# A fused attention and two-stage MoE kernel: earlier query and key loads, a third raw buffer, later reciprocals, and the larger TensorE budget from step 16

## The chip, the cores and the metric

The kernel runs on one core of a Trainium2 chip. The metric is the device time of one execution in microseconds (us), less is better. PE is TensorE, DVE is VectorE, ACT is ScalarE, POOL is GpSimd, and SP is the engine whose queue issues nearly all transfers.

## The reference, cut to what matters

```python
scores = scale * np.matmul(q, k.transpose(0, 1, 3, 2))      # 4 batches, 8 heads, 576 x 576, depth 64
kth = np.partition(scores, -32, axis=-1)[..., -32:-31]
scores = np.where(scores >= kth, scores, -1e9)
attn = np.exp(scores - scores.max(-1, keepdims=True)); attn /= attn.sum(-1, keepdims=True) + 1e-9
x = heads side by side of np.matmul(attn, v)                # 2304 tokens x 512
x = ((x @ w_a) * (x @ w_b)) @ w_out                         # 512 -> 1536 -> 512
# then top 1 of 8 experts by cosine similarity with expert_emb, softmax gate with tau,
out[tokens of e] = gate * (np.maximum(x @ w1[e], 0) @ w2[e])   # 512 -> 1024 -> 512
```

The weights w_a, w_b and w_out come as 64-bit floats, all else as 32-bit floats.

## The kernel before, in words

Attention is cut into 144 rows of 128 queries. DVE finds the 32 largest of each row's 576 scores with four MAX8 and three MATCH_REPLACE8 (lines 385 and 388). A loop over steps walks over the rows: in each step it writes out the scores of the row two ahead, half of the top-k search of the current row and half of that of the one before it, the softmax of the row two back and the transposes ("turn") of the row three or, from step 19 on, four back. On PE, DVE, ACT and POOL the order of the program is the order of execution; only the SP queue is ordered by priority, where a larger offset goes first.

Rows are grouped into parts: four rows of one pair of heads (256 queries of each), five rows where a batch's last 64 queries go with them, or one such row alone (the four parts "0T", rows 48 to 51). A part loads its queries (and, when it is the first of its batch and pair, its keys), splits them into a high and a low half (`split_k`, `split`), and turns them on PE. When its last row is turned, `mix` multiplies the weights `wt` with the values, and `sums` gives the reciprocals of the row sums: POOL adds 1e-9 (line 428), DVE takes the reciprocal (line 430).

Each part takes two `wt` tiles, one for each head, from `WT` buffers: at its first row's turn the first head's and later the other's. A row of "0T" takes both at once, ahead of the `mix` of the part before it, which stands later in the same step.

The three weight matrices are converted during attention, in 36 blocks (`Blocks`): a load into one of `RB` raw buffers, two DVE operations (lines 532 and 534) and one on ACT (535) that read it, an addition on POOL (539), then two copies on ACT and two products on PE. `start` writes out the first three operations, one block every other step up to step 16 and two in each step from then on, with at most two blocks waiting for POOL; `stage` advances the blocks, three times in a step.

As soon as 256 tokens are mixed, they make a group, and `moe1` computes the first MoE for it: 12 blocks of 24 products of 256 columns (line 683) and 6 of 512 (line 652). Nine groups are worked through in the background of attention: PE gets a budget in each step, in nominal us, from which what attention itself takes is subtracted:

```python
share[0] = max((STEP0 if step < S0 else STEP) - cost, 0.0) / max(n, 1)   # 4.5, 38, 5.4
```

Group 0 can't go past a block of weights that isn't written out yet (`yield None`). A group may begin two steps after its last token is written, group 0 one step after; when no group is due, the budget isn't used. After attention come the rest of the groups and the experts.

Of the kernel before, what the change touches and what calls it, by code (L numbers as in the profile page):

```python
# [16 lines left out]
AF = mybir.ActivationFunctionType  # L17
# [18 lines left out]
F0 = 1  # L36
# [4 lines left out]
ZB = 4  # L41
YB = 2
XG = 1
RB = 2
FOLD = (0,)
PEN = (0,)
PC = 512
# [3 lines left out]
STEP0 = 4.5  # L51
D0 = 1
RD = 2
S0 = 38
RGAP = 2
DEBT = 1.0
SB = 5
# [10 lines left out]
FX = (0, 5)  # L68
EK = 1
EL = 1  # L70
WT = 4
QM = 2
AHEAD_P = 5
AHEAD_Q = 2
FG = 100000
# [7 lines left out]
def fused_kernel(  # L83
# [18 lines left out]
    pe, dve, act, pool, sp = nc.tensor, nc.vector, nc.scalar, nc.gpsimd, nc.sync  # L102
# [6 lines left out]
    NE, _, F2 = w1.shape  # L109
    NP = H // 2  # L110
# [52 lines left out]
    eps = cst.tile([P, 1], F32, name="eps")  # L163
# [5 lines left out]

    enT = cst.tile([P, KC, EW], F32, name="enT")  # L170
    dve.memset(enT, 0.0)

    def en_load(mk):
        e_sb = mk.tile([P, RW], F32, name="xr")[:NE, :DM]
# [23 lines left out]
    with ExitStack() as ph:  # L198
# [60 lines left out]
        def load_v(o):  # L259
            o.vs = wk.tile([P, 2, 5, D], F32, name="vs", bufs=2)  # L260
            h0 = 2 * o.pr
            sp.dma_start(
                o.vs[:, :, 0:4, :].rearrange("p h c d -> p h (c d)"),
                v[o.b, h0 : h0 + 2, 0:512, :].rearrange("h (p c) d -> p h (c d)", c=4),
            )
            sp.dma_start(o.vs[64:128, :, 4, :], v[o.b, h0 : h0 + 2, 512:576, :].rearrange("h s d -> s h d"))
# [158 lines left out]
        def sums(o, add):  # L425
            sl = slice(0 if o.M else 4, 5 if o.tail else 4)
            if add:
                pool.tensor_scalar(o.rc[:, sl], o.sm[:, sl], 1e-9, None, op0=OP.add)
                return
            dve.reciprocal(o.rc[:, sl], o.rc[:, sl])  # L430
# [58 lines left out]
        class Blocks:  # L489
# [9 lines left out]
            def fetch(self, n):  # L499
                while len(self.raw) < min(n, len(self.order)):  # L500
# [5 lines left out]
                    if src.dtype == F32:  # L506
                        raw = mk.tile([P, KC, P], F32, name="raw64", bufs=RB)
                        sp.dma_start(raw, src)
# [269 lines left out]
        rows = []  # L778
# [8 lines left out]
        made = {}  # L787

        live = {}
        NRW = len(rows)  # L790
# [73 lines left out]
        for step in range(-AHEAD_L, NRW + TL + 5):  # L864
            now[0] = step
            if step + AHEAD_L < NRW:
                b, pr, part, first, last, kind, c, slot = rows[step + AHEAD_L]
                if first:
                    with tc.high_priority(offset=FG):
                        o = made[b, pr, part] = prep(b, pr, part, len(made), c0)  # L870
                        coming.append(o)
                    if pr == NP - 1:
                        c0 += o.N
            if 0 <= step + AHEAD_P < NRW:
                b, pr, part, first, last, kind, c, slot = rows[step + AHEAD_P]
                o = made[b, pr, part]
                if first:
                    o.flip = turn_qk(o)
                    flips.append(o)
                    parts.append(o)  # L880
                    o.left = 0
                o.left += 1
                live[step + AHEAD_P] = Rows(o, kind, c, slot)
                live[step + AHEAD_P].n = step + AHEAD_P
            for ahead in (1, -2):
                j = step + ahead
                if 0 <= j < NRW and rows[j][3] and (made[rows[j][:3]].n < 2) == (ahead == 1):
                    with tc.high_priority(offset=FG):
                        load_v(made[rows[j][:3]])
            with tc.high_priority(offset=FG):  # L890
                next(soft, None)
                soft = softmax(live[step - 2]) if 0 <= step - 2 < NRW else none
                for back in (3, 5):
                    j = step - back
                    if 0 <= j < NRW and rows[j][4] and (made[rows[j][:3]].n < F0 * NP) == (back == 3):
                        if back == 3:
                            sums(made[rows[j][:3]], True)
                        sums(made[rows[j][:3]], False)
                j = step - 3
                if 0 <= j < NRW and rows[j][4] and made[rows[j][:3]].n >= F0 * NP:  # L900
                    sums(made[rows[j][:3]], True)
                if 0 <= step < NRW:
                    cur = topk(live[step], FOLD[step % len(FOLD)])
                for _ in range(4):
                    next(thresholds[0], None)
                    next(cur, None)
                if step == NRW:
                    thresholds[0] = none
                elif 0 <= step < NRW:
                    thresholds[0] = cur  # L910
            if step == -AHEAD_L:
                conv.fetch(RB)
            pace = {-5: 1, -1: 2}.get(step, 0) if step < 2 else (step + 1) % 2 if step < 16 else 2
            if step == 4:
                e_sb, e_ss = en_load(mk)
            if step == 12:
                en_norm(e_sb, e_ss)
            if step == 14:
                en_turn(mp, e_sb)
            for o in coming[:1]:  # L920
                if step >= o.first - AHEAD_P or (step >= o.first - AHEAD_P - 2 and not flips):
                    pieces.append(split_qk(o))
                    coming.pop(0)
                    while step < EAGER and pieces:
                        piece()
            while 0 <= step + AHEAD_Q < NRW and live[step + AHEAD_Q].o in flips:
                flip_next()
            i = step - (TL0 if step < S1 else TL)
            if i != turned[0] + 1:
                i = -1  # L930
            else:
                turned[0] = i
            tg = turn(live[i]) if 0 <= i < NRW else none
            sg = scores(live[step + AHEAD_Q]) if 0 <= step + AHEAD_Q < NRW else none
            mg = mixes[0] if mixes else none
            cost, n = 0.0, 0
            if tg is not none:
                cost, n = cost + 0.54, n + 2
            if sg is not none:
                cost, n = cost + (0.96 if live[step + AHEAD_Q].kind == 2 else 0.48), n + 2  # L940
            if mg is not none:
                cost, n = cost + parts_n[0] / 100, n + 1
            if flips:
                cost, n = cost + 0.44, n + 2
            share[0] = max((STEP0 if step < S0 else STEP) - cost, 0.0) / max(n, 1)
            for slot_, g in enumerate((tg, sg, tg, mg, sg)):
                if g is not none and not run(g) and g is mg and mixes:
                    mixes.pop(0)
                    mg = none
                with tc.high_priority(offset=FG):  # L950
                    if slot_ == 1 or slot_ == (2 if mg is not none else 3):
                        next(soft, None)
                    if slot_ < 3 and step >= 0:
                        conv.stage()
                if slot_ in (2, 4):
                    piece()
            if 0 <= step + AHEAD_Q < NRW:
                live[step + AHEAD_Q].o.left -= 1
            for _ in range(2):
                flip_next()  # L960
            if 0 <= i < NRW:
                next(tg, None)
                b, pr, part, first, last, kind, c, slot = rows[i]
                t = live.pop(i)
                if last:
                    while mixes:
                        if not run(mixes[0]):
                            mixes.pop(0)
                    mixes.append(mix(t.o))
                    parts_n[0] = t.o.N  # L970
                    while t.o.n < F0 * NP and mixes:
                        if not run(mixes[0]):
                            mixes.pop(0)
            while not EAGER <= step < NRW and pieces:
                piece()
            for _ in range(pace):
                with tc.high_priority(offset=FG):
                    conv.start()
            while done < len(GROUPS) and sum(GROUPS[done]) <= ready[0]:
                w = step + (D0 if done == 0 else RD)  # L980
                todo.append([w, Group(done, w), None])
                if done and len(todo) < 3 and conv.ready(1, NF - 1):
                    todo[-1][1].inputs()
                    if len(todo) == 1:
                        todo[-1][1].load()
                done += 1
# [322 lines left out]
```

## Time and profile before

| | |
|---|---|
| three runs | 1326.34, 1331.99 and 2752.71 us, median 1331.99 |
| profiled execution | 1326.2 us, its span 1324.5 us, mean granted TensorE clock 0.955 |
| busy | PE 1181.9, DVE 913.1, ACT 821.6, POOL 719.9 us |

The span is what the trace shows, from the first instruction to the last; all times in the trace count from its start. A busy PE is not PE at its peak, since matmuls are pipelined. The granted clock is the share of full speed, 2.4 GHz, that the chip lets TensorE run at. Attention ends at about 890 us.

### The profile page before, as it was taken

Reading aid. Unit: us, or ns where it says so; the run is one execution under the profiler, and the core shown is the slowest. Engines: PE = TensorE matmul, PEld = TensorE weight load, DVE = VectorE, ACT = ScalarE, POOL = GpSimd, SP = SyncE. Lnnn points to the kernel's source line nnn. Section 1 sums busy time; section 2 is a strip of 40 time slices with the busy share of each in tenths; the row PEclk is TensorE's granted clock in tenths of the full one; section 3 lists DMA queues with packets and bytes.
Section 4 is the critical chain, followed back from the end, with each engine's and each line's share of the span. In section 5 each row is a group of like instructions: output and inputs, shape, how many; then the busy total and the mean of one; then the engine's idle time right before and its main releaser. Section 6 shows DMA issues by size and latency. Waiting matters only on the chain. (4 is left out here: it accounts for less than half of the span.)

```text
span 1324.5 us, 23353 instructions
## 1 busy us (share of the span) xinstructions
PE 1181.9 (89%) x7908; PEld 996.1 (75%) x7909; DVE 913.1 (69%) x1995; ACT 821.6 (62%) x1961; POOL 719.9 (54%) x1188
## 2 busy tenths in 40 slices
PE   4766988898999987999998998899999989999996
PEld 3544766677898876888887887677898868888885
DVE  6999999988898986999988898750200135444440
ACT  4777888777777775687777776662532334444441
POOL 4555786766677775767766766564445321111100
PEclk9677999999999997999999998899999989999999
DMA  6334476466695654766765667458988145555520
GB/s 211 118 108 140 159 248 219 164 215 211 202 258 166 187 194 135 209 191 195 194 194 175 204 180 211 135 154 268 324 282 253 32 129 198 174 170 168 177 91 19
DMA packets 129101, 240.56 MB, mean 182 GB/s; under 512 B 24621, under 2 KB 73901, under 8 KB 128978
## 3 DMA queue, kind: packets, MB, share of 16 engines
q1 hardware_dynamic: 124818, 228.74, 55.3%
q0 software_dynamic: 4160, 10.29, 2.4%
q8 instruction: 64, 1.05, 0.3%
q14 instruction: 59, 0.48, 0.1%
HBM read 198.92 MB, written 40.85 MB: 181 GB/s over the span
## 5 line engine op out<-in xcount | busy, mean ns | idle before, releaser
L385 DVE MAX8 t<-y 128x8 f32<-128x576 f32 x432 | 312.0, 750 | 2.9
L400 POOL TENSOR_TENSOR z<-s,z 128x576 f32<-128x576 f32 x144 | 206.0, 1430 | 98.0 <-ACT z L397 95.9
L683 PE MATMUL ab<-xg,wab 128*128 128x256 f32 x1440 | 214.4, 291 | 4.8 <-ACT gab L687 3.1
L388 DVE MATCH_REPLACE8 y<-t,y 128x576 f32<-128x576 f32 x288 | 213.9, 743 | 0.0
L683 PEld LDWEIGHTS ab<-xg,wab 128*128 128x128 f32 x1440 | 189.2, 192 | 8.1 <-ACT gab L687 3.5
L683 PE MATMUL ab<-raw,wab 128*128 128x256 f32 x1152 | 173.4, 292 | 7.2 <-ACT gab L687 4.3
L419 PE MATMUL tr<-ident,z 128*128 128x128 f32 x720 | 137.9, 292 | 41.4 <-ACT z L402 34.7
L683 PEld LDWEIGHTS ab<-raw,wab 128*128 128x128 f32 x1152 | 152.2, 193 | 10.7 <-ACT gab L687 5.0
L402 ACT ACTIVATE z<-z,bi 128x576 f32<-128x576 f32 x144 | 111.4, 774 | 78.2 <-POOL z L400 78.0
L385 DVE MAX8 t<-s 128x8 f32<-128x576 f32 x144 | 107.8, 748 | 59.9 <-ACT s L365 49.0
L364 PE MATMUL tr<-kT,qT 128*128 128x288 f32 x512 | 129.2, 336 | 21.5 <-ACT qT L341 10.9
L422 ACT ACTIVATE wt<-tr 128x384 f32<-128x384 f32 (+2 forms) x320 | 127.3, 412 | 18.5 <-PE tr L419 18.0
L365 ACT ACTIVATE s<-tr 128x288 f32<-128x288 f32 x288 | 118.9, 414 | 30.3 <-PE tr L364 28.7
L652 PE MATMUL x<-wo,gh 128*128 128x512 f32 x432 | 137.7, 400 | 0.0
L419 PEld LDWEIGHTS tr<-ident,z 128*128 128x128 f32 x720 | 92.7, 148 | 56.4 <-ACT z L402 38.8
L1015 DVE TENSOR_TENSOR u<-raw,u 128x1024 fp32r<-128x1024 f32 x64 | 76.3, 1221 | 85.3 <-ACT u L1014 62.5
L639 POOL TENSOR_TENSOR gab<-gab 128x256 f32<-128x256 f32 x108 | 81.5, 754 | 97.0 <-ACT gab L687 92.0
L1064 POOL DMA_INDIRECT out_dram<-o,ids x24 | 23.9, 994 | 201.0 <-ACT o L1063 197.7
L1092 PE MATMUL y<-u,hT 128*128 128x512 f32 (+1 forms) x528 | 128.0, 396 | 0.4 <-DVE hT L1197 0.4
L364 PEld LDWEIGHTS tr<-kT,qT 128*128 128x128 f32 x512 | 90.5, 207 | 37.1 <-ACT qT L341 13.2
L397 ACT ACTIVATE z<-s,bi 128x576 f32<-128x576 f32 x144 | 112.5, 781 | 0.0
L1092 PEld LDWEIGHTS y<-u,hT 128*128 128x128 f32 (+1 forms) x528 | 89.7, 174 | 27.6 <-DVE hT L1197 0.5
(178 smaller groups left out, 2213.8 us busy)
## 6 DMA issues: line engine op xcount, KB each, us to landing
wab<-wab_d SPq DMA_DIRECT2D x192, 512.0 KB, 4.4
raw<-in_moe_w_dram SPq DMA_DIRECT2D x28, 1024.0 KB, 5.1
wab_d<-wab SPq DMA_DIRECT2D x24, 512.0 KB, 3.2
kT<-kT_d SPq DMA_DIRECT2D x20, 576.0 KB, 4.5
vs<-in_v_dram SPq DMA_DIRECT2D x36, 256.0 KB, 3.0
kT_d<-kT SPq DMA_DIRECT2D x16, 576.0 KB, 3.7
raw<-in_moe_w_a_dram SPq DMA_DIRECT2D x12, 512.0 KB, 4.1
raw<-in_moe_w_b_dram SPq DMA_DIRECT2D x12, 512.0 KB, 4.3
```

Source lines behind the costliest of these rows:

```text
L364: pe.matmul(p, l, r, start=(i == 0), stop=(i == len(terms) - 1))
L365: act.activation(t.s[:, cs], p, AF.Copy, scale=SCALE)
L385: dve.max(v, cur)
L388: dve.match_replace(out=rest, in_to_replace=v, in_values=cur, imm_value=LOWEST)
L397: act.activation(t.w, t.s, AF.Relu, bias=t.bi[:, 1:2], scale=-HUGE)
L400: pool.tensor_tensor(t.w, t.s, t.w, op=OP.subtract)
L402: act.activation(t.w, t.w, AF.Exp, bias=t.bi[:, 0:1], accum_out=t.o.sm[:, t.slot : t.slot + 1])
L419: pe.transpose(pt[:, i * P : (i + 1) * P], t.w[:, k0 : k0 + P], ident)
L422: act.activation(th[:, sl, w], pv[:, :, src], AF.Copy)
L652: pe.matmul(px[t], g[:, ts], wo[:, w, f], start=(f == 0 and i == 0), stop=(f == NF - 1 and i == 2))
L683: pe.matmul(p[:, i], wt[:, a, c, :], xg[x][:, c, :], start=(j == 0), stop=(j == len(terms) - 1))
L1092: pe.matmul(p[:m], (hi, lo)[a], u[:, b, f % 4, :], start=(f == 0 and i == 0), stop=(f == NF2 - 1 and i == 2))
```

## The change

- The loads of the first three parts get a higher priority on the SP queue than everything else; the value loads of the first two parts come in step 2 after their first row like all others, not in the step before it.
- An activation with Exp on one element stands near the start of ACT's program.
- `RB` is 3 instead of 2 and `WT` 3 instead of 4.
- In the first four parts the reciprocal on DVE is written out in the middle of the step's top-k operations instead of ahead of them.
- `conv.stage` is called from step 2 on, not from step 0.
- `S0` is 16 instead of 38.

```diff
-RB = 2
+RB = 3
-S0 = 38
+S0 = 16
-WT = 4
+WT = 3
     dve.memset(enT, 0.0)
+    act.activation(enT[:, 0, 0:1], eps, AF.Exp)
...
-                    with tc.high_priority(offset=FG):
+                    with tc.high_priority(offset=max(4 - len(made), 1) * FG):
                         o = made[b, pr, part] = prep(b, pr, part, len(made), c0)
...
-            for ahead in (1, -2):
-                j = step + ahead
-                if 0 <= j < NRW and rows[j][3] and (made[rows[j][:3]].n < 2) == (ahead == 1):
-                    with tc.high_priority(offset=FG):
-                        load_v(made[rows[j][:3]])
+            j = step - 2
+            if 0 <= j < NRW and rows[j][3]:
+                with tc.high_priority(offset=FG):
+                    load_v(made[rows[j][:3]])
...
-                for back in (3, 5):
-                    j = step - back
-                    if 0 <= j < NRW and rows[j][4] and (made[rows[j][:3]].n < F0 * NP) == (back == 3):
-                        if back == 3:
-                            sums(made[rows[j][:3]], True)
-                        sums(made[rows[j][:3]], False)
+                j = step - 5
+                if 0 <= j < NRW and rows[j][4] and made[rows[j][:3]].n >= F0 * NP:
+                    sums(made[rows[j][:3]], False)
                 j = step - 3
-                if 0 <= j < NRW and rows[j][4] and made[rows[j][:3]].n >= F0 * NP:
-                    sums(made[rows[j][:3]], True)
+                summed = made[rows[j][:3]] if 0 <= j < NRW and rows[j][4] else None
+                if summed:
+                    sums(summed, True)
                 if 0 <= step < NRW:
                     cur = topk(live[step], FOLD[step % len(FOLD)])
-                for _ in range(4):
+                for n in range(4):
                     next(thresholds[0], None)
                     next(cur, None)
+                    if n == 1 and summed and summed.n < F0 * NP:
+                        sums(summed, False)
...
-                    if slot_ < 3 and step >= 0:
+                    if slot_ < 3 and step >= 2:
                         conv.stage()
```

## Rows read from the trace of the kernel before

**Rows 1.** The page's 40 slices of the span, DVE and granted clock.

```profile
DVE  6999999988898986999988898750200135444440
...
PEclk9677999999999997999999998899999989999999
```

**Rows 2.** Busy time by stretch: length, then each engine, clock, DMA share, GB/s.

```profile
134.00:249.00 115.00, 99.14 (x601) 75.27 (x601) 107.68 (x225) 95.95 (x213) 86.44 (x101) 0.96 0.60 206
249.00:283.00 34.00, 30.39 (x218) 23.65 (x217) 30.62 (x68) 25.90 (x62) 23.15 (x32) 1.00 0.61 204
283.00:483.00 200.00, 187.01 (x1490) 163.69 (x1489) 180.68 (x417) 150.59 (x407) 141.78 (x262) 1.00 0.67 203
```

**Rows 3.** Timeline of the SP queue's issues, first 10 us.

```profile
0.76 0.44 SPq L512 DMA_DIRECT2D raw<-in_moe_w_a_dram  x1
1.26 0.50 SPq L241 DMA_DIRECT2D kr<-in_k_dram  x1
...
3.37 0.57 SPq L246 DMA_DIRECT2D kr<-in_k_dram  x1
...
5.34 0.60 SPq L246 DMA_DIRECT2D kr<-in_k_dram  x1
5.99 3.62 SPq L228 DMA_DIRECT2D qr<-in_q_dram  x4
```

**Rows 4.** The page's transfers: KB each, median us from issue to landing.

```profile
raw<-in_moe_w_a_dram SPq DMA_DIRECT2D x12, 512.0 KB, 4.1
```

**Rows 5.** Timeline of all engines, up to the first MAX8 and shortly after.

```profile
9.54 1.28 ACT L255 ACT_TABLE_LOAD   x1 [9.41 <-DMA kr<-in_k_dram]
...
11.55 1.00 DVE L256 TENSOR_TENSOR ks<-kr,ks 128x576 fp32r<-128x576 f32 x1 [7.94 <-ACT ks L255]
...
14.00 0.42 DVE L532 TENSOR_SCALAR w64t<-raw 128x512 int32<-128x512 int32 x1
...
17.40 0.76 DVE L385 MAX8 t<-s 128x8 f32<-128x576 f32 x1 [1.33 <-ACT s L365]
...
19.61 2.50 POOL L539 TENSOR_TENSOR x1T<-w64t,w64r 128x512 int32<-128x512 int32 x2
```

**Rows 6.** DVE by line, 17 to 110 us: busy, mean ns, idle before.

```profile
L430 DVE RECIPROCAL rc<-rc 128x4 f32<-128x4 f32 x3 | 0.5, 179 | 5.3 <-POOL rc L428 5.3
```

**Rows 7.** DVE by line, 110 to 275 us.

```profile
L385 DVE MAX8 t<-s 128x8 f32<-128x576 f32 x26 | 19.3, 741 | 0.0
L532 DVE TENSOR_SCALAR w64t<-raw 128x512 int32<-128x512 int32 x27 | 15.3, 567 | 7.2 <-DMA raw<-in_moe_w_b_dram 5.2 <-DMA raw<-in_moe_w_a_dram 1.9
```

**Rows 8.** Busy time by stretch, of instructions on tile ab: PE, PEld, ACT.

```profile
140.00:250.00 110.00, 32.66 (x201) 27.46 (x199) 5.42 (x9) 0.97 0.63 216
250.00:290.00 40.00, 9.53 (x64) 8.23 (x64) 1.79 (x3) 1.00 0.63 213
```

**Rows 9.** Timeline of PE, 338 to 342 us.

```profile
338.77 1.59 PE L683 MATMUL ab<-raw,wab 128*128 128x256 f32 x12
...
341.97 0.62 PE L652 MATMUL x<-wo,gh 128*128 128x512 f32 x2
```

**Rows 10.** DVE by line, 275 to 480 us.

```profile
L385 DVE MAX8 t<-s 128x8 f32<-128x576 f32 x36 | 27.0, 751 | 14.9 <-ACT s L365 11.5 <-POOL z L400 2.0 <-POOL gab L639 1.3
```

**Rows 11.** DVE by line, 482.7 to 527.2 us.

```profile
L385 DVE MAX8 t<-s 128x8 f32<-128x576 f32 x6 | 4.5, 758 | 10.3 <-ACT s L365 10.3
```

**Rows 12.** Busy time by stretch, 500 to 517 us.

```profile
500.00:517.00 17.00, 13.30 (x64) 10.08 (x63) 11.15 (x25) 9.98 (x24) 10.38 (x20) 0.61 0.28 67
```

**Rows 13.** Timeline of PE and ACT in the steps that turn 0T.

```profile
347.59 2.53 PE L460 MATMUL tr<-wt,vs 128*64 128x256 f32 x20
...
348.58 0.53 ACT L422 ACTIVATE wt<-tr 128x192 f32<-128x192 f32 x2
...
353.87 0.55 ACT L422 ACTIVATE wt<-tr 128x192 f32<-128x192 f32 x2
...
355.44 0.89 PE L460 MATMUL tr<-wt,vs 128*64 128x64 f32 x18
...
359.15 0.55 ACT L422 ACTIVATE wt<-tr 128x192 f32<-128x192 f32 x2
...
361.64 0.89 PE L460 MATMUL tr<-wt,vs 128*64 128x64 f32 x18
```

## The prediction

> **What bounds the kernel now.** I read the 40 slices first, then busy time by stretch, and then, for each stretch that the change touches, the DVE rows by line and what ended the idle time before them. The slices show DVE nearly full up to the end of attention, with a dip at the 16th slice where the granted clock dips too [rows 1]. By stretch there are two regimes. From 134 to 249 us DVE is busy 107.7 of 115 us and PE 99.1: DVE sets the pace, because the weight blocks are converted in it, and PE has some 16 us to spare. From 283 to 483 us PE is busy 187.0 of 200 us and DVE 180.7, and DVE's idle time there ends with scores from ACT [rows 2, 10]: PE's queue sets the pace. So a DVE wait that is taken away before about 250 us moves everything behind it earlier, as long as PE keeps up; PE work that is moved counts only where PE is the bound.
>
> **The start.** SP issues in the order of the rows: the three key loads lie behind and between raw weights and values, the last at 5.34 us, and the query loads begin at 5.99 [rows 3]. ACT gets the keys at 9.5 us, loads its table for 1.28 us, copies, and DVE subtracts at 11.55 [rows 5]. With keys and queries first, the three key loads take 0.50, 0.57 and 0.60 us of issue from 0.76 on, so the last begins at 1.83 instead of 5.34 us: 3.5 us earlier, and with the table already loaded the subtraction comes 3.5 + 1.3 = 4.8 us earlier. But what moves back is the raw block. DVE's order has its first operation on raw weights at 14.00 us, ahead of the last copies before the first MAX8 at 17.40 [rows 5]. Behind three key loads (1.67 us) and four query loads (3.62 us) the first raw load is issued at 0.76 + 5.29 = 6.05 us and lands, by the median of its kind, 4.1 us later [rows 3, 4], at 10.15: 3.85 us ahead of 14.00. So the raw weights are late next, and the first MAX8 comes at about 13.5 us. **Term: -3.9 us.** The bounds are -4.8 (the raw lands sooner, the key chain decides) and -2.5 (I allow it 1.4 us more, since the queries and keys are still being moved).
>
> **Loads and stages moved.** The value loads of the first two parts leave the head of the SP queue for step 2 of their part; the first `mix` is four steps later, which hides them. If that cover were gone, the mix would wait one landing, of the size of that in [rows 4], twice. Starting `stage` at step 2 delays the additions and copies of two blocks; nothing needs these blocks before group 0 in step 21. The third block's DVE operation then waits for a free buffer that POOL gives back in step 2; if DVE reaches it first, it loses one addition of about 1.25 us (two take 2.50) [rows 5]. The first three parts' higher priority can hold SP only at a key buffer that the first part hasn't freed, and the loads behind it are needed later. All of this at nothing.
>
> **Reciprocals.** In the first four parts DVE stands still until POOL has added to the row sums: 5.3 us before three of them [rows 6]. Put behind four of the step's DVE operations of 0.74 us each (as a MAX8) [rows 7], some 3 us, the reciprocal finds its input ready, as the three waits are 5.3/3 = 1.8 us in the mean. The order on PE is unchanged: `along`, which reads the reciprocals, stands behind `mix`. **Term: -5.0 us**, between -5.3 and -3, if scores are late next.
>
> **The third raw buffer.** From 110 to 275 us DVE waits 7.2 us for raw weights before line 532, 27 blocks [rows 7], while MAX8 never waits for scores (0.0). A buffer is free when DVE and ACT have both read it, and the next load is written out only then. With three buffers the load goes out one block earlier, and in most steps that is one step earlier, more than its landing of about 4 us. The upper end is all 7.2 us; the lower is nothing, since PE is at 86% in this stretch and gets more to do (next). **Term: -4 us**, the middle.
>
> **The budget from step 16.** Group 0 begins in step 21. I followed the loop's counters through these steps (cost of each generator, share, debt of at most 1, blocks written out): before, its 288 products of 256 columns are all written out by step 39, after by step 35, and the gate `yield None` turns the background away only five times. That 64 of these products lie in the trace behind 250 us, 201 between 140 and 250 [rows 8], agrees with the first count. What moves ahead is then about 64 products and 16 of 512 columns. Twelve of 256 took 1.59 us, 0.12 each with the pipeline's end subtracted, two of 512 took 0.62, some 0.2 each [rows 9]: 7.7 + 3.2 = 11 us of PE. The room for it is the 16 us that PE idles between 134 and 249 [rows 2].
>
> Where it is taken away it gives little. From 249 to 283 us DVE is busy 30.6 of 34 us, so at most 3.4 us can be had there. Behind that the budget of each step is as before; groups 1 and 2 end two steps sooner, but group 1 may not begin before step 40 and group 3 not before step 80, since the attention rows set these dates, and the budget that finds no group is lost. Nor are such steps quick: in the gap ahead of group 3, six steps take 44.5 us, 7.4 each, with DVE idle 10.3 us for scores [rows 11], against 205/36 = 5.7 us a step with the budget in use [rows 10]. So two more empty steps there may cost 2 x 1.7 = 3.4 us. **Term: 0**, from -3.4 to +14 (+3.4, and +10 for a second gap, see the rivals).
>
> **Three wt buffers.** Only 0T's rows take two buffers at once. With three, the second copy of the row must wait for the `mix` of the part before, which PE reaches later. In the trace these copies begin at 348.6, 353.9 and 359.2 us, the first of each pair taking some 0.27, and those mixes end at 350.1, 356.3 and 362.5 [rows 13]: waits of 1.3, 2.2 and 3.1 us, with a fourth row some 9 us of ACT's queue, and behind it the scores for the next row. Scores are made two rows ahead, and ACT is busy three quarters of the time in such steps (150.6 of 200 us) [rows 2], so most is caught up. **Term: +2 us**, from 0 to +6. Four- and five-row parts take their second buffer two rows later, when that mix is done: nothing.
>
> **Sum.** -3.9 - 5.0 - 4 + 0 + 2 = -10.9 us. From the profiled 1326.2 us (span 1324.5 and 1.7 around it) that gives 1315. That run stands 5.8 us below the median of the three runs shown and at their lowest; a median after may stand a little over its fastest too, so I say 1316.
>
> **Rivals.** *The moved work pays in full:* if steps behind 283 us lose 11 us of PE work one for one, because PE is the bound there, the time is 1315 - 11 = 1304. For it speaks PE's 187 of 200 us; against it, that the step's budget stays the same and the gap ahead of group 3 already swallows what is done early. *The emptied gap:* slower. Group 0 ends in step 35 to 38 and group 1 starts in step 40, so there is a new gap of some four steps of the kind in [rows 11]. In that gap's second half the granted clock is 0.61, between its two levels of 1.2 and 2.4 GHz, after PE had been partly idle [rows 12], and the next group starts at the low level. Six steps times 1.7 us is 10 us; with the longer gap ahead of group 3 (+3.4) and the full +6 for 0T, against -12.9 of the first three terms: +6.5, or 1333 us. It decides from the point where the clock falls in the new gap; against it speaks that the four-row parts around step 36 leave PE less of a chain to wait for, and that products of 512 columns trickle on to step 38. The Trainium skill has a rule on this side ("TensorE: Matmul & The Clock Gate", section on HAM oscillation): bursts of matmuls with waits between them let the clock fall back, and every next burst starts cold. The trace agrees at this one gap (0.61); by the rule the time would be this rival's. *The change does not do what it says:* the third buffer brings nothing, as ACT reads the raw block late and PE fills up, scores hold DVE where the reciprocal did (-3), the start gives -2.5 and 0T takes +6: +0.5, 1327 us.
>
> **How the numbers follow.** Forecast 0.50, full payment 0.17, emptied gap 0.18, not what it says 0.15. The range runs from 1302 to 1335: down to just past full payment, and up past the gap, with what is left out at its ends under 0.2. Two per cent, about what can be told from no change here, is 26.6 us of 1332: under 1305 lies half of the full payment, with the other half and the tail of the forecast above it, so 0.08; over 1358 the gap would have to open twice, 0.05; within 0.87.
>
> **What would show it.** The first MAX8 at 13 to 14 us; no idle time before the early reciprocals; the idle time before line 532 under 4 us; group 0's last product of 256 columns at about step 36; ACT waiting on PE before line 422 only around step 52; a granted clock of 1.00 between steps 36 and 41 for the forecast, one under 0.9 for the emptied gap. The prediction is wrong if the raw loads hold DVE much past 10 us, if DVE starts to wait for scores from 134 us on, or if steps in the budgeted stretch take other than 5.7 us.

## The result, and the profile after

The change made the kernel slower: 1336.26 us in the median of six runs beside 1327.8 us of the kernel before, a ratio of 1.0067 [1.0048, 1.0087], in brackets its 95% interval. That is 8.9 us more, where 1316 us was forecast, and just outside the range, which ended at 1335. One of the six runs of before, of 2752.71 us, is left out of the ratio. The profiled execution took 1340.65 us (span 1338.9), 4.4 above that median, so the worth of a whole edit is taken from timed ratios below; lengths of steps come from one trace each and show places.

To see where, I read the times at which steps begin (the MAX8 on `s` opens a step). The shift against before is -3.2 us at step 0, -4.7 at step 22, +6.1 at step 34, +5.6 at 36, +13.3 at 44, +14.2 at 53, +18.0 at 58, +14.0 at 84 and +14.4 at the end. So the loss arises between steps 22 and 58, and nothing behind step 84 plays a visible part.

The 40 slices of the page, after, answer to [rows 1]:

```profile
DVE  7999998879878998899989899760110135444440
...
PEclk8876999978999998999999999799999989999999
```

The clock's dip in the 16th slice is smaller than before (8 for 7), and there is a new one in the 9th, 268 to 301 us (7 for 9); DVE has digits of 7 and 8 in most of slices 7 to 13. Where the time goes is told by stretches. Busy time by stretch, after (length, then PE, PEld, DVE, ACT, POOL, clock, DMA share, GB/s); the first row is that of [rows 2], the second is steps 22 to 34, the others run through steps 37 to 41:

```profile
134.00:249.00 115.00, 98.88 (x602) 72.64 (x602) 105.64 (x206) 92.97 (x201) 84.17 (x96) 0.99 0.60 207
...
140.00:242.90 102.90, 89.53 (x538) 64.11 (x537) 93.64 (x180) 82.77 (x178) 75.88 (x85) 1.00 0.65 227
...
260.00:268.00 8.00, 8.00 (x60) 5.79 (x60) 5.45 (x12) 5.85 (x16) 5.06 (x10) 1.00 0.57 176
268.00:276.00 8.00, 3.43 (x24) 2.87 (x22) 4.89 (x12) 5.13 (x14) 3.92 (x9) 0.95 0.21 83
276.00:281.00 5.00, 4.53 (x18) 3.98 (x18) 5.00 (x13) 3.34 (x9) 3.23 (x10) 0.50 0.67 212
281.00:286.00 5.00, 2.88 (x17) 2.70 (x17) 4.97 (x12) 4.65 (x11) 4.11 (x6) 0.50 0.33 96
286.00:295.00 9.00, 9.00 (x56) 6.21 (x55) 5.61 (x13) 3.60 (x11) 3.12 (x6) 0.65 0.11 29
```

and the same twelve steps of before:

```profile
144.70:236.80 92.10, 77.07 (x471) 56.15 (x470) 84.88 (x176) 78.15 (x171) 70.57 (x80) 0.98 0.67 229
```

In the fixed window 134 to 249 after looks like before (PE 98.9 against 99.1 us), which says only that both kernels work at the same rate there. Taken by steps, the same twelve rows of attention last 102.9 instead of 92.1 us. PE is busy 12.5 us more in them, and its idle time stays: 13.4 us after, 15.0 before. What PE waits for shows in its rows by line, steps 22 to 34, after (busy, mean ns of one, idle before; after's line numbers are one higher than before's):

```profile
L551 PE MATMUL tr<-x1T,ident 128*128 128x512 f32 x48 | 25.8, 618 | 7.8 <-POOL x1T L540 7.7
...
L552 PE MATMUL tr<-wab,minusr 128*128 128x512 f32 x18 | 12.2, 680 | 2.9 <-ACT wab L548 2.8
...
L552 PE MATMUL tr<-wo,minusr 128*128 128x512 f32 x6 | 3.9, 647 | 2.6 <-ACT wo L548 2.6
```

These are the two products of the conversion of a weight block, waiting for POOL's addition and ACT's copy of that block: 13.3 of the 13.4 us. Before, in the same steps, the wait ahead of them is shorter, and PE also waits for the queries that the scores are made from:

```profile
L550 PE MATMUL tr<-x1T,ident 128*128 128x512 f32 x37 | 19.3, 600 | 2.1 <-POOL x1T L539 2.1
L364 PE MATMUL tr<-kT,qT 128*128 128x288 f32 x50 | 12.1, 317 | 4.8 <-ACT qT L341 4.2 <-ACT wt L422 0.7
...
L551 PE MATMUL tr<-wab,minusr 128*128 128x512 f32 x13 | 8.6, 659 | 4.9 <-ACT wab L547 4.9
```

With 1.6 us ahead of the same product for `wo`, the conversion has 8.6 of before's 15.0 us, and other waits have 6.4. So the "16 us to spare" of the prediction were two things. After, the other waits are gone, and those for the conversion have grown by 4.7 us: PE works in program order, and its queue stands behind a product whose input isn't ready, whatever else is written out behind it.

DVE's conversion rows in the same stretch, after:

```profile
L535 DVE TENSOR_SCALAR w64r<-raw 128x512 int16<-128x512 int16 x22 | 18.9, 860 | 0.0
L533 DVE TENSOR_SCALAR w64t<-raw 128x512 int32<-128x512 int32 x22 | 18.4, 836 | 9.2 <-POOL x1T L540 6.8 <-DMA raw<-in_moe_w_b_dram 2.4
```

Beside [rows 7], raw weights hold DVE little now (2.4 us); it waits for POOL instead, and one operation of line 533 takes 0.836 us where it took 0.567 (0.603 in these twelve steps alone).

### The profile page after: what moved, and what is told of

Read it like the earlier page. It is cut to its first block, busy times and chain, and to the rows that moved or that the text cites. A ratio compares the mean times of both kernels' runs of the same rounds, so it can differ in the third digit from the quotient of the medians.

```text
span 1338.9 us, 23347 instructions
## 1 busy us (share of the span) xinstructions
PE 1187.8 (89%) x7908; PEld 998.4 (75%) x7909; DVE 921.8 (69%) x1995; ACT 820.1 (61%) x1962; POOL 721.1 (54%) x1188
## 5 line engine op out<-in xcount | busy, mean ns | idle before, releaser
L684 PE MATMUL ab<-xg,wab 128*128 128x256 f32 x1440 | 210.9, 289 | 5.5 <-ACT gab L688 3.4
L423 ACT ACTIVATE wt<-tr 128x384 f32<-128x384 f32 (+2 forms) x320 | 127.6, 412 | 27.7 <-PE tr L420 18.8
L420 PEld LDWEIGHTS tr<-ident,z 128*128 128x128 f32 x720 | 93.1, 149 | 57.2 <-ACT z L403 37.7
```

The source lines that it names most:

```text
L420: pe.transpose(pt[:, i * P : (i + 1) * P], t.w[:, k0 : k0 + P], ident)
L423: act.activation(th[:, sl, w], pv[:, :, src], AF.Copy)
L684: pe.matmul(p[:, i], wt[:, a, c, :], xg[x][:, c, :], start=(j == 0), stop=(j == len(terms) - 1))
```

## The experiments

The first theory was that the budget from step 16 (S0) alone loses the time, in the conversion of weights or in the gap it opens between groups 0 and 1; the rivals were the third raw buffer and the third `wt` buffer. Step starts (us) of the runs that are spoken of, worked out from the MAX8 rows:

| run | step 0 | 22 | 34 | 36 | 44 | 53 | 58 | 84 | end |
|---|---|---|---|---|---|---|---|---|---|
| before | 17.4 | 144.7 | 236.8 | 249.2 | 294.7 | 345.9 | 377.6 | 532.4 | 1324.5 |
| after | 14.2 | 140.0 | 242.9 | 254.8 | 308.0 | 360.1 | 395.6 | 546.4 | 1338.9 |
| e1 | 14.2 | 141.0 | 231.5 | 247.6 | 293.1 | 344.2 | 379.9 | 534.6 | 1325.8 |
| e2 | 18.8 | 145.7 | 251.8 | 262.6 | 316.6 | 367.6 | 400.2 | 548.8 | 1341.2 |
| e7 | 14.1 | 140.5 | 244.5 | 255.3 | 309.1 | 360.1 | 392.9 | 542.8 | 1331.5 |
| e8 | 13.9 | 139.7 | 241.7 | 253.5 | 304.5 | 356.9 | 392.8 | 542.3 | 1330.9 |
| e10 | 14.3 | 144.1 | 238.5 | 250.8 | 296.3 | 347.4 | 379.2 | 534.1 | 1332.7 |
| e11 | 14.0 | 137.7 | 231.5 | 241.7 | 289.9 | 342.4 | 379.5 | 531.4 | 1320.9 |
| e12 | 12.9 | 139.1 | 227.1 | 241.1 | 281.8 | 333.2 | 368.5 | 523.4 | 1314.8 |
| e13 | 10.3 | 142.0 | 234.7 | 248.1 | 292.2 | 343.5 | 375.2 | 529.9 | 1321.5 |
| e16 | 14.3 | 140.6 | 241.7 | 253.5 | 303.0 | 354.9 | 389.0 | 538.5 | 1330.8 |

**e1_s0_38**, all of the change but the budget; **e2_only_s0_16**, the budget alone, on the kernel before.

```diff
-S0 = 16      (e1, on after)
+S0 = 38
...
-S0 = 38      (e2, on before)
+S0 = 16
```

> The changed kernel with S0 back at 38, all else as changed. Theory A (the earlier budget costs the time: it crowds the weight conversion between steps 22 and 34 and opens a gap between groups 0 and 1 in which the clock falls): the head's 4.7 us stay gained and the 19 us lost behind step 22 come back, so about 9 us under the kernel before, ratio 0.993. Theory B (the third raw buffer crowds the conversion): still some 10 us slow in steps 22 to 34, ratio 1.003 or more. Theory C (three wt buffers): ratio not under 1.000, steps 52 to 60 slow.

> The kernel before with S0 at 16 alone. Theory A: 10 to 19 us slower than before, ratio 1.008 to 1.014, with the gap and the fallen clock around step 38. Theories B and C: within 3 us of before, ratio 0.998 to 1.002.

Measured: e1 0.9995 [0.9978, 1.0013], e2 1.0073 [1.0047, 1.0099]. Both ways S0 costs the same: 1.0067 - 0.9995 = 0.0072, or 9.6 us, and 9.7 us. It is the loss, whatever the other parts are. All the rest together gives nothing measurable, where the forecast had -10.9. Theory A's 0.993 for e1 didn't come: the time that S0 loses came back, but steps 53 to 58 stayed slow, which is theory C's sign (more on it below).

Where raw weights come from two buffers, the early budget shows its cost at another place. DVE in steps 22 to 34 of e2, whose length is 106.1 us:

```profile
L532 DVE TENSOR_SCALAR w64t<-raw 128x512 int32<-128x512 int32 x22 | 15.1, 685 | 19.5 <-DMA raw<-in_moe_w_a_dram 13.2 <-DMA raw<-in_moe_w_b_dram 3.5 <-DMA raw<-in_moe_w_out_dram 2.7
```

So with three buffers DVE waits less there (9.2 us in all), but the loss is the same.

**e3_two_raw** and **e7_two_raw_wt4**, after with the buffers of before: first the raw ones, then both.

```diff
-RB = 3
+RB = 2
...
-WT = 3      (e7 alone)
+WT = 4
```

> The changed kernel with two raw buffers. Theory A: within 4 us of the changed kernel, ratio 1.004 to 1.010 to before, DVE waiting for raw weights again instead of for POOL. Theory B: steps 22 to 34 take 92 us as before, not 103, and the ratio is near 0.998.

> The changed kernel with two raw buffers and four wt buffers; beside the run with two raw buffers and three it shows what the fourth wt buffer is worth. Theory A: within 2 us of that run. Theory C: at least 4 us faster than it, won between steps 52 and 60.

Measured: 1.0093 [1.0075, 1.0111] and 1.0073 [1.0048, 1.0098]. Neither wins the loss back, so neither trade is its cause. Steps 53 to 58 last 35.5 us after, 35.9 in e3 and 32.8 in e7: with four `wt` buffers the 0T rows cost some 3 us less. That is between the 2 us at most of theory A and the 4 at least of theory C.

**e11_noprod_16** and **e12_noprod_38**: is it PE's queue or the conversion ahead of it? Both leave out the two products of each block on PE (the low half is a plain copy, so the weights and what follows from them are other numbers); S0 is 16 and 38.

```diff
-                p = ps.tile([P, 512], F32, name="tr", bufs=NTR)
-                pe.matmul(p, ident, x.rearrange("p c j -> p (c j)"), start=True, stop=False)
-                pe.matmul(p, minusr, hi.rearrange("p c j -> p (c j)"), start=False, stop=True)
-                act.activation(lo, p.rearrange("p (c j) -> p c j", c=KC), AF.Copy)
+                act.activation(lo, x, AF.Copy)
```

> The changed kernel without the two PE products of each weight block: the low half is a copy of the block by ACT, so the first MoE's result is off. Theory A1 (in steps 22 to 34 PE's queue is full with its waits for the conversion, and every moved product lengthens them): steps 22 to 34 take within 3 us of the same kernel with S0 at 38. Theory A2 (the conversion chain on DVE, ACT and POOL is the limit): at least 8 us more than with S0 at 38, as with the products.

> The same with S0 at 38. Both theories: steps 22 to 34 take 84 to 90 us, the reference for the run with S0 at 16.

Measured, in one execution each: 1322.67 and 1316.55 us. Steps 22 to 34 of e11:

```profile
137.70:231.50 93.80, 71.73 (x477) 57.51 (x475) 92.82 (x180) 84.06 (x185) 78.22 (x88) 0.95 0.71 250
```

and of e12:

```profile
139.00:227.00 88.00, 64.16 (x421) 52.37 (x420) 87.97 (x176) 78.47 (x176) 74.03 (x83) 0.90 0.71 246
```

With the products, S0 costs 102.9 - 90.5 = 12.4 us here; without them, 93.8 - 88.0 = 5.8, which neither theory had. The 5.8 us are DVE's, which is full in both rows: 22 blocks instead of 20 are written out (two operations of 0.41 and 0.46 us each, 1.7 us), 0.9 us is idle, and the operations take 3.4 us more in sum beside POOL (the last section says more). But these two blocks are not additional work: with S0 at 38, DVE has them in steps 34 to 36. Up to step 36, where all four runs have converted the same blocks, S0 costs 114.8 - 106.6 = 8.2 us with the products and 104.0 - 102.0 = 2.0 without. So most of what is lost up to there goes with PE's two products, as theory A1 had it, while steps 36 to 44 stay 7.5 us longer without them (48.2 and 40.7). Whether it is the products' own time or the waits ahead of them, these runs don't tell, as both go together; and the granted clock differs between the two (0.95 and 0.90).

**e8_fill** and **e14_fill12**: does the clock that falls in the new gap cost the time there? After, with four and with twelve products of 128 columns, identity by identity, written out with each share of the budget that finds no group due, several times in a step; their result isn't used.

```diff
             debt[0] = min(debt[0] + budget, DEBT) if not final else final
+            if 22 <= now[0] < NRW and not (todo and todo[0][0] <= now[0]):
+                w = mp.tile([P, 512], F32, name="ab", bufs=2)
+                for j in range(4):      # e14: range(12), column block j % 4
+                    pe.matmul(w[:, j * P : (j + 1) * P], identr, identr, start=True, stop=True)
```

> The changed kernel, and wherever no group is due from step 22 on, PE gets four products of the identity with itself (128 columns, result unread) in place of each share of the budget. Theory D (the gaps cost because the granted clock falls in them): the clock stays at 1.00 in steps 36 to 42, these six steps take at most 34 us instead of 39.7, steps 133 to 139 at most 38 instead of 41.5, and the time comes to 8 to 12 us under the changed kernel, ratio to before about 0.998. Rival (the gaps cost by their chain of waits alone): clock up or not, no step gets shorter, ratio 1.007 or more.

> The changed kernel with twelve filling products instead of four in each share that has no group due. Theory D (clock): the granted clock stays at 1.00 through steps 36 to 42, which take at most 34 us. Rival (chain of waits, and products that stand in PE's way): 38 us or more, whatever the clock.

Measured: e8 1.0017 [0.9991, 1.0043], 6.6 us better than after; e14, in one execution, 1375.18 us. But steps 36 to 44 took 51.0 us in e8 (53.2 after), so only 2.2 us of the gain lies in that gap, and in e14 they took 73.4. Busy time by stretch in e8, from step 38 on:

```profile
274.10:280.90 6.80, 5.88 (x28) 5.88 (x28) 6.32 (x15) 4.89 (x14) 4.94 (x12) 0.50 0.59 193
280.90:291.00 10.10, 10.10 (x92) 8.56 (x91) 8.97 (x20) 7.41 (x19) 5.65 (x9) 1.00 0.14 40
```

and in e14:

```profile
272.00:286.00 14.00, 12.77 (x60) 12.77 (x61) 10.33 (x23) 5.78 (x15) 6.34 (x14) 0.51 0.40 116
286.00:296.00 10.00, 10.00 (x51) 10.00 (x50) 2.79 (x7) 2.64 (x6) 2.64 (x4) 0.50 0.02 3
```

In e8 the granted clock is 0.50 for 6.8 us, where it is for 17 us after, and the gap is 2.2 us shorter. So ten us less at the lower clock went with 2.2 us: the fall of the clock looks like a small part of what this gap costs, though what the filling itself takes is not told apart. Steps 36 to 42 took 37.5 us, more than theory D's 34, and the rival, with no step shorter and 1.007, isn't right either. Some 4 us of e8's gain lie behind step 84 in its trace; why is not shown. In e14 PE is full and yet the clock stays at its lower level, 1.2 GHz, for longer: twelve filling products take 2.65 to 2.80 us there, and 1.45 to 1.56 at 1.00 in the gap ahead of group 3. But there too they make the steps longer (77 to 82 take 55.4 us, after 37.7), so twelve are too many at either clock, and e14 gives no price for the clock alone.

**e16_late_pow**: the other thing in the gap. When group 0 is done, its router starts in step 37. The timeline, after, around step 38 (time, duration, engine, line; in brackets idle time before it and what ended it):

```profile
271.00 0.63 ACT L719 ACTIVATE x1T<-xr 128x512 f32<-128x512 f32 x1
...
271.87 0.58 POOL L720 TENSOR_TENSOR st<-st,half 128x1 f32<-128x1 f32 x1 [3.73 <-ACT x1T L719]
...
273.13 1.40 POOL L401 TENSOR_TENSOR z<-s,z 128x576 f32<-128x576 f32 x1
...
274.56 0.77 ACT L403 ACTIVATE z<-z,bi 128x576 f32<-128x576 f32 x1 [2.84 <-POOL z L401]
...
275.63 0.59 ACT L342 ACTIVATE qT<-tr 128x512 fp32r<-128x512 f32 x1
275.83 0.76 DVE L386 MAX8 t<-s 128x8 f32<-128x576 f32 x1 [3.08 <-ACT s L366]
...
276.26 0.61 PE L365 MATMUL tr<-kT,qT 128*128 128x288 f32 x1 [4.83 <-ACT qT L342]
```

It is read from the bottom up: PE waits 4.83 us for queries that ACT copies late, as ACT waited 2.84 us for POOL's softmax operation, which stood in POOL's queue behind the router's `pow`, a few numbers that waited 3.73 us for ACT's square. So a one-column operation holds three engines here. e16 moves the router's three POOL operations behind a `yield`, one turn of the background later:

```diff
+            yield 0.0
             pool.tensor_tensor(st[:, 1:2], st[:, 0:1], half, op=OP.pow)
...
             pool.tensor_tensor(st[:, 1:2], st[:, 1:2], tau1, op=OP.mult)
-            yield 0.0
```

> The changed kernel with the router's first three operations on POOL written out one stage later, so that they no longer wait for ACT ahead of the softmax. Theory E (this wait stops PE at the end of group 0 and so brings the clock down): POOL's 3.7 us wait ahead of the power goes, step 38 takes under 6.5 us instead of 8.3, the clock falls later or not at all before step 41, and steps 37 to 43 take at least 4 us less. Rival (PE simply has nothing to do in the gap): step 38 shorter by at most 2 us, the clock falls all the same, and steps 39 to 43 are as slow.

Measured: 1.0021 [0.9995, 1.0046], 6.1 us better than after. What POOL waited for ahead of this operation in the whole span (us, times), after:

```profile
  ACT x1T L719: 19.9, 10
```

and in e16:

```profile
  ACT x1T L719: 5.0, 4
```

Step 38 lasts 5.5 us instead of 8.3, and steps 36 to 44 take 49.6 instead of 53.2, so about half of the 7.7 us by which they are longer than before was this wait. That is theory E's wait, but the rival's clock: it fell all the same (at 273.9 us, for 13.7 us), and steps 41 to 43 stayed slow (21.1 us, 22.0 after). What is left against before lies in step 37 (2.6 us), in which PE is full (8.00 us of 8 in the row of 260 to 268), and in step 42 (2.9 us), which is not explained.

**e10_head**, **e13_head_latestart**, **e9_head_fill** and **e15_s0_30**: the change without S0 and without the buffer trade (RB = 2, WT = 4), that is, the early loads, the Exp, the later reciprocals and `stage`; then with the first weight blocks begun in step 1, behind the start; with the filling of e8; and with S0 at 30.

```diff
-S0 = 16      (e10; e15: 30)
+S0 = 38
-RB = 3
+RB = 2
-WT = 3
+WT = 4
...
-            pace = {-5: 1, -1: 2}.get(step, 0) if step < 2 else ...      (e13 alone)
+            pace = {1: 2}.get(step, 0) if step < 2 else ...
```

> The changed kernel with S0 at 38, two raw and four wt buffers: only the early loads, the Exp, the later reciprocals and stages are left of the change. If the head's gain of 3 to 5 us in the first 20 steps stays (nothing behind it takes it back): ratio 0.996 to 0.998. If later stretches take it back, 1.000. No ACT wait before line 423 around step 52.

> The same, with the first two weight blocks begun in step 1 and not in steps -5 and -1, so that their raw weights stand behind the first MAX8 in DVE's order. If the raw weights are what holds the first MAX8 at 14 us: it comes at 10.5 to 11.5 us, and 2.5 to 3.5 us are won over the run before. If the keys and queries hold it, it stays at 14.

> The changed kernel with S0 at 38, two raw and four wt buffers (so only the head, the reciprocals and the later stages stay), and the same fillings of steps with no group due. Theory D: the gaps ahead of groups 3 and 6 get 5 to 8 us shorter together, and with the 4 us of the head ratio 0.990 to 0.993. Rival: 0.997, the head alone.

> The head's kernel (two raw, four wt buffers) with S0 at 30. Theory A (each product moved ahead lengthens steps 22 to 34, since PE has no free time there): steps 22 to 30 as with S0 at 38, steps 30 to 34 longer by 2 to 4 us, a smaller gap. Rival (only the blocks that are written out two steps earlier cost): nearly all of the 12 us, or none.

Measured: e10 0.9966 [0.9949, 0.9983], e13 0.9939 [0.9919, 0.996], e9 0.9927 [0.9902, 0.9952]; e15, in one execution, 1331.82 us. The head of the change alone makes the kernel 4.5 us faster, and the blocks begun later about 3.6 more, though the two intervals overlap. e9 has the lowest ratio of all, within what theory D said, but not for its reason: the gaps ahead of groups 3 and 6 (steps 77 to 82 and 133 to 138) take 44.5 and 41.3 us in its trace, beside 44.6 and 41.0 in e10. Why the filling helps here stays open. In e15 steps 22 to 34 last 100.3 us, 5.9 more than in e10, all of it from step 30 on; up to step 36 it is 3.7, where 22 steps of early budget with the same buffers (e7) cost 8.1. The profiled execution of e10 took 1334.5 us, some 11 above the median of its runs, and lost some 7 us behind step 140, so its trace doesn't show where the 4.5 us lie.

e7 less e10 is a third price of S0, with the new head and the buffers of before: 1.0073 - 0.9966 = 0.0107, or 14.2 us. So S0 costs 10 to 14 us, by what stands beside it and with some 3 us of noise in each price.

**e17_head_late_pow**, e13 with the edit of e16:

> The kernel with early loads, later reciprocals, S0 at 38, two raw buffers, four wt buffers and the first weight blocks begun in step 1, with the same later router operations. Theory E: 0.5 to 1.5 us less at the end of each of the eight groups, ratio to before 0.985 to 0.992. Rival: 0.994, as without.

Measured: 0.996 [0.9945, 0.9974], no better than e13. POOL's wait ahead of `pow` falls here as well, 15.0 to 5.0 us in the span, and gains nothing that can be told: steps 36 to 44 take 44.0 us in both, and only the gap ahead of group 6 is shorter (38.9 us, 41.0 in e13). So this wait costs where a gap exposes it; that PE has other work while it lasts elsewhere is my reading.

## Why the prediction was wrong, point by point

**The budget, forecast 0 (-3.4 to +14), measured +9.6 (+14.2 by e7 less e10).** This is the step that failed, in its sentence "the room for it is the 16 us that PE idles between 134 and 249". The counting was right: group 0's last product of 256 columns starts at 259.9 us, at the end of step 36, as said, and PE has 12.5 us more to do in steps 22 to 34. But PE's idle time is still 13.4 us with the additional work in it. Only the 6.4 us that ended with other work took any; the rest was waits in a chain (DVE, POOL, ACT, PE) for each weight block, and grew from 8.6 to 13.3 us. Whether idle time in an in-order queue takes work depends on what the work is written out in front of. I also left out that the same edit writes out two weight blocks earlier, on a DVE that I had named as the bound there. What is given back is small: 4.2 us between steps 34 and 36, where those two blocks were, so that 8.2 us are lost up to step 36, most of it with PE's products (e11, e12). Behind step 44 it is 3.1 us up to step 84 (after less e1): steps 44 to 76 take 3.7 us more, and the gap ahead of group 3, which I let grow by 3.4 us, shrank by 6.7 (steps 77 to 82 take 37.7 us, in e1 44.4).

**The emptied gap, a rival at 0.18.** It came, at its place: steps 36 to 44 take 53.2 us after, 45.5 before and in e1, and the granted clock is 0.50 from 275.2 us on for 17 us. The forecast's row, a clock of 1.00 between steps 36 and 41, didn't hold. By its result (1333) this rival is the nearest of the four, but that is in part luck: it had only the 7.7 us of the gap, not the 8.2 up to step 36, and its sum held -12.9 us for the first three terms, where the head gave -4.5 and the third buffer some -3.5 at most, and +3.4 for the gap ahead of group 3, which shrank. About half of the 7.7 us was POOL's queue, which no rival had (e16), and some 2 went with the clock (e8). The Trainium skill ("TensorE: Matmul & The Clock Gate", section on HAM oscillation) says that the clock falls when matmuls come in bursts with waits between. The trace agrees: PE is busy 3.43 of 8 us and waits 4.83 us at one place where the clock falls.

**The start, forecast -3.9, measured -3.2.** The issues on the SP queue, after, answer to [rows 3]:

```profile
0.76 0.44 SPq L242 DMA_DIRECT2D kr<-in_k_dram  x1
1.26 1.20 SPq L247 DMA_DIRECT2D kr<-in_k_dram  x2
2.50 2.01 SPq L229 DMA_DIRECT2D qr<-in_q_dram  x4
4.55 0.44 SPq L513 DMA_DIRECT2D raw<-in_moe_w_a_dram  x1
...
5.56 0.38 SPq L242 DMA_DIRECT2D kr<-in_k_dram  x1
...
8.24 0.43 SPq L513 DMA_DIRECT2D raw<-in_moe_w_b_dram  x1
```

and DVE's operations answer to [rows 5]:

```profile
4.77 0.76 DVE L257 TENSOR_TENSOR ks<-kr,ks 128x576 fp32r<-128x576 f32 x1 [1.16 <-ACT ks L256]
...
8.64 0.43 DVE L533 TENSOR_SCALAR w64t<-raw 128x512 int32<-128x512 int32 x1 [1.57 <-DMA raw<-in_moe_w_a_dram]
...
13.44 0.49 DVE L533 TENSOR_SCALAR w64t<-raw 128x512 int32<-128x512 int32 x1 [3.43 <-DMA raw<-in_moe_w_b_dram]
14.19 0.74 DVE L386 MAX8 t<-s 128x8 f32<-128x576 f32 x1
```

The subtraction comes 6.8 us earlier, not 4.8, and raw weights are late next, as forecast, but the second block, not the first: it is issued behind the next part's keys and holds DVE 3.43 us. In e13, where the blocks begin later, the first MAX8 is

```profile
10.34 0.76 DVE L386 MAX8 t<-s 128x8 f32<-128x576 f32 x1 [2.03 <-ACT s L366]
```

3.9 us earlier still, though steps 0 to 2 then take 12.2 us instead of 9.0, so that 0.8 us of it is left at step 2. The mechanism was right; only which block is late was not.

**Reciprocals, forecast -5.0, measured between nothing and some -2.** The row of [rows 6], after, steps 0 to 17:

```profile
L431 DVE RECIPROCAL rc<-rc 128x4 f32<-128x4 f32 x3 | 0.5, 178 | 1.9 <-POOL rc L429 1.9
```

3.4 us of waiting went, but steps 0 to 22 became only 1.5 us shorter (127.3 to 125.8, from the table). Half of what was taken away turned up again in DVE's conversions, which take 5.0 us over the 0.41 and 0.46 us of the short ones in these steps, 3.3 before. They are long beside POOL, as in these rows of steps 6 and 7, after:

```profile
47.21 0.18 DVE L431 RECIPROCAL rc<-rc 128x4 f32<-128x4 f32 x1 [0.36 <-POOL rc L429]
...
49.55 1.61 POOL L401 TENSOR_TENSOR z<-s,z 128x576 f32<-128x576 f32 x1 [1.44 <-ACT z L398]
49.80 1.66 DVE L535 TENSOR_SCALAR w64r<-raw 128x512 int16<-128x512 int16 x1
51.36 0.74 DVE L386 MAX8 t<-y 128x8 f32<-128x576 f32 x1
```

A conversion of 0.46 us takes 1.66 us: it starts 0.25 us behind POOL's operation and ends 0.30 behind its end. And the later place alone doesn't take the wait away. In e10, where it stands beside two raw buffers, the same three reciprocals wait 6.1 us, and steps 0 to 22 last 129.8:

```profile
L431 DVE RECIPROCAL rc<-rc 128x4 f32<-128x4 f32 x3 | 0.5, 178 | 6.1 <-POOL rc L429 6.1
```

The sum of the three waits is 0.0 to 1.9 us in the traces with three buffers (after, e1, e8, e14, e16) and 1.0 to 6.8 in those with two (e3, e7, e9, e10, e13, e15, e17). So "the reciprocal finds its input ready" failed there: POOL's addition itself waits, in e10 4.6 us for ACT's softmax.

**The third raw buffer, forecast -4, measured some -3.5, not clear of noise.** That is after less e3 (1.0067 - 1.0093), whose intervals overlap. It came in other steps than forecast. In e1, with three buffers and the old budget, steps 22 to 34 show:

```profile
L533 DVE TENSOR_SCALAR w64t<-raw 128x512 int32<-128x512 int32 x20 | 17.3, 866 | 2.0 <-DMA raw<-in_moe_w_a_dram 1.0 <-POOL x1T L540 0.8 <-DMA raw<-in_moe_w_out_dram 0.2
```

The waits fell as forecast, 7.2 to 2.0 us (before's twelve steps have all 7.2), but the operations became longer (before 11.3 us over the 0.41 and 0.46 us that they take alone, e1 14.9), and steps 34 to 36 gave 3.7 us back. There its own rival, that it "brings nothing", was right, for another reason. What differs is steps 0 to 22, which last 124.1 to 126.8 us in the five traces with three buffers named above and 126.4 to 131.7 in the seven with two. Why the buffers matter to the reciprocals' wait there is not shown.

**Three `wt` buffers, forecast +2 (0 to +6), measured about +4.** ACT's copies in the 0T rows of e1 wait for PE:

```profile
348.50 0.33 ACT L423 ACTIVATE wt<-tr 128x192 f32<-128x192 f32 x1 [1.26 <-PE tr L461]
...
355.49 0.33 ACT L423 ACTIVATE wt<-tr 128x192 f32<-128x192 f32 x1 [2.22 <-PE tr L461]
```

1.26 and 2.22 us, beside 1.3 and 2.2 worked out from [rows 13], and a third of 3.2 (forecast 3.1). Their sum is 6.7 us, and steps 53 to 58 last 35.6 us beside 31.7 before and in e10: 3.9 us are not caught up, where I took 2. The mechanism was right. Taking both buffer trades back at S0 = 38 gives 0.9995 - 0.9966 = 0.0029, or 3.9 us, with some 3 us of noise; at S0 = 16 (e7 and after) it gives nothing that can be told apart.

**Sum.** -4.5 (head and reciprocals, e10) + 3.9 (buffers, e1 less e10) + 9.6 (budget, after less e1) = +9.0 us, beside 8.9 measured. This agrees by construction, as each run ends one term and begins the next, and is no proof of the shares. The other way round, by e7, it is -4.5 + 14.2 (budget) - 0.8 (buffers) = 8.9. Either way the loss is the budget's.

## What to carry to other kernels

Before work is moved into an engine's idle time, see what ends each part of that time: here the waits inside the chain of the weight blocks were no room and grew, while the others were filled, and the place that the work came from became a gap with its own price. Count all that an edit moves (here two weight blocks as well), not only the part that its name speaks of. And a wait that is taken away on one engine is gained only if what moves up doesn't stand still beside another engine: half of the reciprocals' gain went into longer conversions beside POOL.

## What the runs showed of the hardware

**Long conversions on DVE end with POOL.** The two conversions take from 0.403 and 0.436 us (least) to 1.482 and 1.711 (most) in the trace after. The long ones in steps 22 to 34 (over 0.15 us more than the 0.41 and 0.46 us) all end 0.28 to 0.34 us behind the end of a POOL operation, as in the rows of step 7: 17 of 17 before, 21 of 21 in e1 and 23 of 23 after. Of the short ones, 6 of 23, 8 of 19 and 9 of 21 end within their own 0.41 or 0.46 us of such an end. The Trainium skill ("SBUF — State Buffer", section "SBUF: two separate sides") says that DVE in some of its modes and GpSimd share a port pair, which whoever starts first holds for the whole instruction. The trace agrees with that pattern; no run here took POOL's work away to prove it. In sum the conversions take 11 to 18 us more in these twelve steps than they would if all were short.

**A busy PE at the lower clock.** In e14 the granted clock was 0.50 for 37.5 us from 272 us on, while PE worked through products of 128 columns almost without idle time. In e8, with four products instead of twelve at the same place, it was 0.50 for 6.8 us. And in e14, in the gap ahead of group 3, it stayed at 1.00 with the same filling. The filling products of the first of these, by line, 272 to 309 us (108 of them, 0.413 us each; from 528 to 575 us, in the other gap, 228 of them, 0.275 us each):

```profile
L800 PE MATMUL ab<-identr 128*128 128x128 f32 x108 | 24.6, 413 | 0.0
```

In the first gap PE had stood still for 4.85 us and the clock had fallen, at 272.2 us, before the filling began at 273.6; in the other the clock was at 1.00 when it began. What else tells these cases apart, and why the clock came back sooner with fewer products, is open.
